# A block-sparse attention with a routed mixture of experts on one core: the third chunk's products one step later, PSUM halves alternating by pair, another opening

## The chip, the cores and the metric

One core of a Trainium2 chip (trn2) runs the whole program. The metric is the device time of one execution in microseconds (us); lower is better. Engines are named as the profile names them: PE is TensorE's matmul, PEld its weight load, DVE is VectorE, ACT is ScalarE, POOL is GpSimd, SP is SyncE, whose queue issues most DMAs.

## The reference: what is computed

Attention over 4 batches, 8 heads, 768 positions of 64 values, all float32. A block of 32 queries sees its own block of 32 keys and the two neighbours, the first and the last block, and 3 sampled blocks; the first and the last query block see everything. Then each of the 3072 rows (8 heads side by side, 512 values) is routed to one of 8 experts with a two-layer network.

```python
mask = np.abs(blk_i - blk_j) <= window
mask = mask | (blk_i == 0) | (blk_j == 0) | (blk_i == n_blocks - 1) | (blk_j == n_blocks - 1)
for qb in range(n_blocks):
    for kb in sampled_blocks[qb]:
        mask[qb * block:(qb + 1) * block, kb * block:(kb + 1) * block] = True
...
attn = np.exp(scores)
attn = attn / (np.sum(attn, axis=-1, keepdims=True) + 1e-09)
...
h = np.maximum(x_sorted[lo:hi] @ w1[e], 0.0)
y_sorted[lo:hi] = h @ w2[e]
return (gate_w[:, None] * y).astype(np.float32)
```

## The kernel before, in words

The program is one stream written out by hand for PE, DVE, POOL, ACT and SP. It opens with the loads and transposes of batch 0, then runs 48 attention steps, then the experts' tiles of 128 rows.

**Groups and steps.** A batch has six groups. Five (numbers 0 to 4) hold 128 query rows, which are two tiles of 64 (`ti` 0 and 1). The sixth, `GL`, comes first in each batch and has one tile of 64 rows, and beside it the 64 rows of the first and the last query block, which see all 768 keys. A group takes two steps, one for each half of the heads; a half is two pairs `pr` of heads, and `hh` is the head in a pair. So there are 4 x 6 x 2 = 48 steps, and the list `steps` gives their order.

**What a step does.** Step i makes the scores of its two pairs (`scores`, L357; for the rows that see everything L349) into a PSUM tile, ACT takes the exponential into a buffer `ea` (L362), DVE multiplies with the mask (L368, for `GL` L372). PE then transposes keys or queries of the next batch (`turn`, L178) and, in every second step, finished rows for the routing (`turn_out`, L469). Then come the products with V of the step before: `attend` (L388 on) for an ordinary group, `attend_last` for `GL`; both go through `product` (L383 to L390, the matmul is L386). After them come the routing logits (`logits`, L492) of a finished group, and `divide` on DVE (L445, L447, L451), which frees the PSUM bank.

**Chunks.** The keys of a tile lie in three chunks of 128: chunk 0 is the end blocks and the middle, chunks 1 and 2 are gathered. Their values of V come into the tile `around` (two sets, used in turn by `parity`), by POOL's indirect DMA from the copy `v_rows` in DRAM (`fetch_values(b, g, ti, ch)`, L525: `ch` 0 fills chunk 1, `ch` 1 fills chunk 2). Before most of them POOL copies one element of another tile (`not_before`, L539), so that the fetch is not issued too early. The rows of the two end blocks come by SP's DMA (`fetch_ends`, L535), rows of V of the own tile by copies on ACT and DVE (`place_values`, L544 and L545), keys by copies into `kr` and `xk` (`place_keys`, L567 and L570; `place_middle`, L551 and L552).

**PSUM halves.** A product has 64 output partitions: tile 0 writes partitions 0 to 63 of its bank, tile 1 partitions 64 to 127. In `attend` the two tiles alternate from one matmul to the next. In `GL` the 64 ordinary rows (three chunks) are half 0 and the rows that see everything (six chunks) half 1; `attend_last` alternates for three chunks and then runs the other three on half 1 alone. In batch 0 the rows that see everything are done in the opening, all on half 1 (`attend_all`, called four times), and the ordinary rows of `GL` later, all on half 0. There are two such banks (`ps_o`, 2 buffers); three score tiles (`ps_s`); seven buffers `ea`.

A float32 matmul of the program is two MATMUL records in the trace.

Of the kernel before, what the change touches and what calls it, by code (L numbers as in the profile page):

```python
# [17 lines left out]
def kernel(  # L18
# [11 lines left out]
    nc = tc.nc  # L30
# [351 lines left out]

    def product(b, g, pr, ti, hh, e, values, last):  # L383
        bank, begun = bank_of(b, g, pr)
        op = bank[:, : 4 * (D + 4)].rearrange("p (r h w) -> p r h w", r=2, h=2)
        nc.tensor.matmul(  # L386
            op[ti * D : (ti + 1) * D, pr % 2, hh, : D + 1], lhsT=e, rhs=values[:, (2 * pr + hh) * VW : (2 * pr + hh + 1) * VW],
            start=ti not in begun, stop=last, skip_group_check=True,  # L388
        )
        begun.add(ti)  # L390

    def attend(units_):

        for ch in range(3):
# [6 lines left out]
    def attend_all(b, pr, e, chunks):  # L401
        for c in chunks:
            for hh in range(2):
                product(b, GL, pr, 1, hh, e[:, hh, c * D : (c + 1) * D], sets[b][2][:, c, :], c == NCH - 1)

    def attend_last(b, pr, e_all, e_two):
        for ch in range(3):
            for hh in range(2):
                x = 3 * (pr % 2) + ch
                product(b, GL, pr, 0, hh, e_two[:, hh, x * D : (x + 1) * D], values_of(b, GL, 0, ch), ch == 2)  # L410
                if e_all is not None:
                    product(b, GL, pr, 1, hh, e_all[:, hh, ch * D : (ch + 1) * D], sets[b][2][:, ch, :], False)
        if e_all is not None:
            attend_all(b, pr, e_all, range(3, NCH))
# [19 lines left out]
    for pr in range(NPR):  # L434
        attend_all(0, pr, es[("all", pr)], range(NCH))
# [5 lines left out]
    def divide(b, g, half):  # L441
# [13 lines left out]
        if half == 1:  # L455
            for p, n, row in pieces(g):
                nc.sync.dma_start(x_d[b * S + row : b * S + row + n, :DM], xb[p : p + n, :])
# [26 lines left out]
    def logits(b, g, beside=None):  # L484
        xo = xos.pop((b, g))
        if beside is not None:
            lg = banks_of[beside][0][:, 4 * (D + 4) : 4 * (D + 4) + E]
        else:
            lg = ps_o.tile([P, E], F32, name="lgl", tag="op")[:]
        for c in range(DB):  # L490
            for j in range(2):
                nc.tensor.matmul(  # L492
                    lg[j * D : (j + 1) * D, :], lhsT=xo[:, c * P + j * D : c * P + (j + 1) * D], rhs=wg[:, c, :],
                    start=(c == 0), stop=(c == DB - 1), skip_group_check=True,
                )
# [812 lines left out]
    fetch_ends(0, GL)  # L1308
# [5 lines left out]
    fetch_ends(0, 0)  # L1314
# [6 lines left out]
    steps = [(b, g, half) for b in range(B) for g in order for half in range(2)]  # L1321
    for i, (b, g, half) in enumerate(steps):
# [15 lines left out]
        if two:  # L1338
# [17 lines left out]
        if half == 1 and i + 1 < len(steps):  # L1356
            not_before(mine[1][4][0:1, 0, 0:1])
            fetch_values(*steps[i + 1][:2], 0, 1)

        copy_turned = None  # L1360
        if b + 1 < B:
# [3 lines left out]
            if 2 <= here < 10:  # L1365
                copy_turned = turn(b + 1, (here - 2) // 2, here % 2, None, (here - 2) // 2 % 2)
                if 4 <= here < 8:
                    fill_next(b + 1, here)
# [3 lines left out]
        out_of = steps[i - 3][:2] if i >= 3 and half == 1 else None  # L1372
# [4 lines left out]
        if i > 0 and before[0][1] != GL:  # L1377
            attend(before)
        elif i > 0:
            for b_, g_, pr, e_all, e in before:  # L1380
                attend_last(b_, pr, e_all, e)
        if "gates" in rt:
            gate_weights()
        if out_of:
            logits(*out_of, beside=steps[i - 1])
            if out_of[1] == order[-1]:
                gate(out_of[0])
        if i > 0:
            divide(*steps[i - 1])
        early(late)  # L1390
        if half == 0 and nxt is not None:
# [195 lines left out]
```

## Time and profile before

| what | value |
|---|---|
| median of 3 runs | 640.93 us (637.01 to 645.84) |
| the profiled execution's own time | 638.06 us |
| its span | 636.3 us |
| granted TensorE clock over the span | 0.995 of full speed |
| PE busy / PEld busy | 608.2 us / 516.0 us |
| DVE / ACT / POOL busy | 315.6 / 231.9 / 193.8 us |

The span is cut in the prediction into the opening up to the first product (0 to 20.44 us), the attention steps (20.44 to 278.50 us) and the experts (278.50 to 629.3 us). A row of the timeline gives a start, a length, the engine, the line and the tiles, the count, and in brackets the idle time of the engine just before with what ended it. The starts of two neighbouring rows are the safe measure of how long PE takes for something, since the ends of matmuls are modelled.

### The profile page before, as it was taken

How to read it: one execution, taken by the hardware profiler on the slowest of the kernel's cores; microseconds unless marked ns; L12 is line 12 of the kernel's file. 1: busy time of each engine (PE TensorE's matmuls, PEld its weight loads, DVE VectorE, ACT ScalarE, POOL GpSimd, SP SyncE). 2: the span in 40 equal slices, each digit the busy share in tenths (PEclk: the TensorE clock that was granted, in tenths of full speed). 3: DMA queues.
4: the chain of work that ended last, by engine and by line, in shares of the span. 5: the costliest groups of instructions: out<-in, count | busy, mean ns of one | idle time of the engine just before them, and what ended most of it. 6: DMA issues, size and time to landing. Idle time of an engine off the chain costs nothing. (4 is left out here: it accounts for less than half of the span.)

```text
span 636.3 us, 20201 instructions
## 1 busy us (share of the span) xinstructions
PE 608.2 (96%) x8326; PEld 516.0 (81%) x8326; DVE 315.6 (50%) x1025; ACT 231.9 (36%) x456; POOL 193.8 (30%) x289
## 2 busy tenths in 40 slices
PE   6899999999999899999999999999999999999994
PEld 6888999998989899997777776877878787967862
DVE  7477767675778567635852485303190118203300
ACT  5376766665667577721111011111112111111110
POOL 2157745643456445720111221011401130020110
PEclk9899999999999999999999999999999999999999
DMA  8899966995696657899999999869998999769710
GB/s 264 207 193 246 288 162 153 255 261 154 136 247 206 184 147 250 261 322 369 338 305 313 344 388 336 303 229 379 396 399 281 365 399 399 291 205 407 299 40 20
DMA packets 125061, 170.86 MB, mean 269 GB/s; under 512 B 71236, under 2 KB 71237, under 8 KB 124934
## 3 DMA queue, kind: packets, MB, share of 16 engines
q1 hardware_dynamic: 114896, 137.61, 66.3%
q0 software_dynamic: 10000, 31.59, 16.0%
q8 instruction: 75, 1.23, 0.8%
q14 instruction: 52, 0.43, 0.2%
q10 hardware_dynamic: 38, 0.00, 0.0%
HBM read 150.11 MB, written 19.33 MB: 266 GB/s over the span
## 5 line engine op out<-in xcount | busy, mean ns | idle before, releaser
L525 POOL DMA_INDIRECT around<-v_rows,rows_of x88 | 100.0, 1136 | 55.3 <-DMA around<-v_rows 21.2
L362 ACT ACTIVATE ea<-s 128x768 f32<-128x768 f32 x104 | 83.6, 811 | 83.2 <-PE s L357 56.1
L1119 DVE STREAM_TRANSPOSE around<-xg 32x128 f32<-32x128 f32 x192 | 58.1, 303 | 86.9 <-DMA xg<-x_rows,gB 81.9
L1138 PEld LDWEIGHTS hp<-around,room 128*128 128x128 f32 x832 | 94.7, 192 | 3.9 <-issue 3.2
L1138 PE MATMUL hp<-around,room 128*128 128x128 f32 x832 | 96.8, 276 | 0.6 <-issue 0.3
L386 PE MATMUL op<-around,ea 128*64 128x65 f32 x2112 | 85.5, 224 | 8.8 <-DMA around<-v_rows,rows_of 5.1
L386 PEld LDWEIGHTS op<-around,ea 128*64 128x64 f32 x2112 | 75.4, 137 | 15.5 <-DMA around<-v_rows,rows_of 6.1
L368 DVE TENSOR_TENSOR ea<-ea,mask 128x768 f32<-128x768 f32 x80 | 74.6, 955 | 14.7 <-ACT ea L362 10.1
L1152 PE MATMUL zp<-room,kr 128*128 128x512 f32 x176 | 77.6, 594 | 0.0
L1145 ACT ACTIVATE kr<-hp 128x512 f32<-128x512 f32 x36 | 21.4, 597 | 116.0 <-PE hp L1138 98.3
L1172 POOL DMA_INDIRECT out_dram<-kr,sB x14 | 14.1, 1008 | 160.2 <-ACT kr L1162 97.9
L1152 PEld LDWEIGHTS zp<-room,kr 128*128 128x128 f32 x176 | 32.6, 190 | 37.2 <-issue 37.2
L357 PE MATMUL s<-other,kr 64*128 64x128 f32 x704 | 48.1, 272 | 0.3 <-issue 0.3
L357 PE MATMUL s<-room,kr 64*128 64x128 f32 x704 | 47.9, 272 | 0.2 <-issue 0.2
L1138 PEld LDWEIGHTS hp<-around,other 128*128 128x128 f32 x384 | 43.8, 192 | 2.3 <-issue 2.3
L1138 PE MATMUL hp<-around,other 128*128 128x128 f32 x384 | 44.3, 275 | 0.0
L357 PEld LDWEIGHTS s<-other,kr 64*128 64x128 f32 x704 | 43.7, 188 | 0.6 <-issue 0.6
L357 PEld LDWEIGHTS s<-room,kr 64*128 64x128 f32 x704 | 43.7, 188 | 0.0
L1250 DVE STREAM_TRANSPOSE ea<-ea 32x128 f32<-32x128 f32 x84 | 21.7, 285 | 30.9 <-DMA ea<-x_rows,gB 30.2
L1162 ACT ACTIVATE kr<-zp,xg 128x512 f32<-128x512 f32 x12 | 8.2, 687 | 74.9 <-PE zp L1152 74.9
L1152 PE MATMUL zp<-other,kr 128*128 128x512 f32 x80 | 35.3, 593 | 0.0
L1119 DVE STREAM_TRANSPOSE around<-kr 32x128 f32<-32x128 f32 x48 | 14.5, 302 | 36.3 <-PE hp L1138 34.9
(369 smaller groups left out, 831.2 us busy)
## 6 DMA issues: line engine op xcount, KB each, us to landing
room<-in_moe_w_dram SPq DMA_DIRECT2D x30, 2048.0 KB
other<-in_moe_w_dram SPq DMA_DIRECT2D x16, 2048.0 KB
room<-in_moe_w_dram SPq DMA_DIRECT2D x16, 512.0 KB
x_rows<-xb SPq DMA_DIRECT2D x20, 256.0 KB
room<-in_k_dram SPq DMA_DIRECT2D x24, 192.0 KB
room<-in_q_dram SPq DMA_DIRECT2D x24, 192.0 KB
v_rows<-room SPq DMA_DIRECT2D x12, 260.0 KB
v_rows<-other SPq DMA_DIRECT2D x12, 260.0 KB
```

The costliest lines, as they stand in the source:

```text
L357: nc.tensor.matmul(s[:, hh, a : a + P], lhsT=keys(r), rhs=moving, start=True, stop=True)
L362: nc.scalar.activation(e, s[:, :, : 6 * D], AF.Exp, scale=scale)
L368: nc.vector.tensor_tensor(e, e, m[:, None, :].to_broadcast([P, 2, 6 * D]), op=ALU.mult)
L386: nc.tensor.matmul(op[ti * D : (ti + 1) * D, pr % 2, hh, : D + 1], lhsT=e, rhs=values[:, (2 * pr + hh) * VW : (2 * pr + hh + 1) * VW], sta ...
L525: nc.gpsimd.indirect_dma_start(out=around[p0:, par, 1 + ti + 2 * ch, :], out_offset=None, in_=v_d[b][:, :], in_offset=bass.IndirectOffsetO ...
L1119: nc.vector.transpose(xT[d, :, t], xg[t, :DM].rearrange("p (c q) -> p c q", c=DB)[:, :, d])
L1138: nc.tensor.matmul(hp[:, m, :], lhsT=st[i]["w1"][:, c, fb * P : (fb + 1) * P], rhs=st[i]["xT"][:, c, :], start=(c == 0), stop=(c == DB - 1),)
L1145: nc.scalar.activation(hT[:, g * (FB // 2) : (g + 1) * (FB // 2), :], hp[:], AF.Relu)
L1152: nc.tensor.matmul(zp[:], lhsT=st[i]["hT"][:, fb, :], rhs=st[i]["w2"][:, fb, :], start=(fb == 0), stop=(fb == FB - 1),)
L1162: nc.scalar.activation(zo, zp[:], AF.Copy, scale=of_i)
L1172: ins = nc.gpsimd.indirect_dma_start(out=to[:, :], out_offset=bass.IndirectOffsetOnAxis(ap=at, axis=0), in_=rows, in_offset=None, bounds_c ...
L1250: nc.vector.transpose(xT_u[d, :, j * P + tq * 32 : j * P + (tq + 1) * 32], xg_u[t, j, :DM].rearrange("p (c q) -> p c q", c=DB)[:, :, d],)
```

## The change

Four things are changed.

- **The third chunk a step later.** For the steps where `in_two` holds (ordinary groups, but for the last step of each batch and the last four of all) `attend` is called twice: chunks 0 and 1 of step i-1 and then, one step later, chunk 2. In a step chunk 2 of step i-2 comes first, then chunks 0 and 1 of step i-1. A half is divided after its third chunk, so one step later; the finished rows are transposed at three steps behind the group's last (`out_at`), in even steps where it was odd ones. The fetch of chunk 2 of tile 0 is issued behind the products of step i-2, since it overwrites what they read.
- **Halves by pair.** In `GL` the ordinary rows of an odd pair now use half 1 and the rows that see everything half 0 (`side_of`), so that `in_turns` can alternate the halves to the end: 18 products on each side of a step for batches 1 to 3, 6 on each for batch 0, 12 on each for two pairs of the opening. The rows are written out to DRAM in two pieces of 256-byte runs each, and `logits` reads the swapped side.
- **The opening.** The scores of steps 0 to 3 come ahead of the products of steps 0 and 1, which both run in step 3. The transposes for batch 1 begin a step later.
- **End rows on chip.** For the first two groups the end blocks' values are copied by POOL from the loaded V, in place of four SP DMAs that read `v_rows` again.

```diff
+    def side_of(g, pr, ti):
+        return (ti + pr) % 2 if g == GL else ti
     def product(b, g, pr, ti, hh, e, values, last):
...
-            op[ti * D : (ti + 1) * D, pr % 2, hh, : D + 1], lhsT=e, ...
+            op[side * D : (side + 1) * D, pr % 2, hh, : D + 1], lhsT=e, ...
...
+    def in_turns(*sides):
+        for two in zip(*sides, strict=True):
+            for one in two:
+                product(*one)
+    def attend_last(units_):
+        sides = [[], []]
+        for b, _, pr, _, e_two in units_:
+            sides[pr % 2] += of_last(b, pr, e_two)
+        for b, _, pr, e_all, _ in units_:
+            if e_all is not None:
+                sides[1 - pr % 2] += of_all(b, pr, e_all)
+        in_turns(*sides)
...
-    for pr in range(NPR):
-        attend_all(0, pr, es[("all", pr)], range(NCH))
+    for half in range(2):
+        attend_first((2 * half, 2 * half + 1))
...
-    fetch_ends(0, GL)
+    for g in order[:2]:
+        for j in range(2):
+            nc.gpsimd.tensor_copy(
+                around[j * BLK : (j + 1) * BLK, parity(0, g), 0, :],
+                sets[0][2][j * (P - BLK) : j * (P - BLK) + BLK, j * (NCH - 1), :],
+            )
...
+    def in_two(n):
+        return steps[n][1] != GL and n % (2 * NG) != 2 * NG - 1 and n < len(steps) - 4
+    out_at = {}
+    for n in range(1, len(steps) - 2, 2):
+        out_at[n + (3 if n < len(steps) - 4 else 2)] = steps[n][:2]
...
-            if 2 <= here < 10:
+            turned_ = here - (2 if b else 3)
+            if 0 <= turned_ < 2 * NPR:
...
-        if i > 0 and before[0][1] != GL:
-            attend(before)
+        if i == 3:
+            for n in range(2):
+                attend_last(units_of[n])
+                divide(*steps[n])
...
+        if i > 1 and in_two(i - 2):
+            attend(units_of[i - 2], range(3) if i == 4 else (2,))
+            closed.append(i - 2)
+            spare = banks_of[steps[i - 2]][0]
+            if not out_of:
+                divide(*steps[i - 2])
+        if half == 1 and i + 1 < len(steps):
+            not_before(mine[1][4][0:1, 0, 0:1])
+            fetch_values(*steps[i + 1][:2], 0, 1)
+        if i > 3:
+            if steps[i - 1][1] == GL:
+                attend_last(units_of[i - 1])
+            else:
+                attend(units_of[i - 1], (0, 1) if in_two(i - 1) else (0, 1, 2))
```

How the instructions stand on PE at three places. A row is a line, the operation, the tiles, the output's size and the count; here one product counts once. First the opening, from the products of the rows that see everything (48) on; `s` are scores, `op` products, `tp` the transposes for batch 1. Minus is before, plus after.

```order
-L386 MATMUL op<-room,ea 64x65 x48
+L390 MATMUL op<-room,ea 64x65 x48
 L357 MATMUL s<-room,xk 128x128 x2
 L357 MATMUL s<-room,kr 128x128 x4
...
-L386 MATMUL op<-around,ea 64x65 x12
+L357 MATMUL s<-room,xk 128x128 x2
+L357 MATMUL s<-room,kr 128x128 x8
+L357 MATMUL s<-room,xk 128x128 x2
+L357 MATMUL s<-room,kr 128x128 x8
```

The 48 products keep their place and count (only which half comes after which is changed, which the rows don't show); behind the scores of steps 0 and 1 stood 12 products of step 0, and now the scores of step 2 stand there.

Second, the products of batch 0 at steps 4 to 6 with the semaphores that they wait for: DMASW are POOL's fetches, DVE the masks and divisions. Before, steps 5 and 6:

```order
L386 MATMUL op<-around,ea 64x65 x8
L386 MATMUL op<-around,ea 64x65 [waits DMASW6_49]
L386 MATMUL op<-around,ea 64x65 [waits DMASW7_49]
L386 MATMUL op<-around,ea 64x65 x6
L386 MATMUL op<-around,ea 64x65 [waits DMASW0_49]
L386 MATMUL op<-around,ea 64x65 [waits DMASW1_49]
L386 MATMUL op<-around,ea 64x65 x6
L492 MATMUL op<-wg,xo 64x8 [waits Activation_49]
```

Now, steps 5 and 6:

```order
L390 MATMUL op<-around,ea 64x65 x8
L390 MATMUL op<-around,ea 64x65 [waits DVE_49,PE_49]
L390 MATMUL op<-around,ea 64x65 x7
L390 MATMUL op<-around,ea 64x65 [waits DMASW6_49]
L390 MATMUL op<-around,ea 64x65 [waits DMASW7_49]
L390 MATMUL op<-around,ea 64x65 x6
...
L390 MATMUL op<-around,ea 64x65 [waits DMASW0_49]
L390 MATMUL op<-around,ea 64x65 [waits DMASW1_49]
L390 MATMUL op<-around,ea 64x65 x22
```

The two waits for the chunk 2 fetches (DMASW0 and DMASW1) stood 16 products behind the first of step 5; now they stand at the head of the products of step 6. In step 5 the ninth product, the first into the next bank, waits for DVE's division.

Third, the second `GL` step of batch 1; `other` is V of that batch for the rows that see everything, `around` the gathered V.

```order
-L386 MATMUL op<-around,ea 64x65
-L386 MATMUL op<-other,ea 64x65
-L386 MATMUL op<-around,ea 64x65
-L386 MATMUL op<-other,ea 64x65 x7
+L390 MATMUL op<-around,ea 64x65 x12
+L390 MATMUL op<-other,ea 64x65 x24
```

Before, each of the two pairs ended with six products in a row on one half (seven rows of `other`, the first of them still beside its partner); now all 36 alternate between the halves, the 12 of `around` first.

## Rows read from the trace of the kernel before

**Rows 1.** Stretches of the span: us, then busy us and count of PE, PEld, DVE, ACT, POOL, the granted PE clock, the DMA share and GB/s.

```profile
20.44:278.50 258.06, 244.60 (x5725) 233.34 (x5722) 173.32 (x522) 167.27 (x336) 136.90 (x210) 1.00 0.81 210
278.50:629.30 350.80, 348.46 (x2287) 268.93 (x2286) 127.27 (x461) 52.78 (x99) 51.34 (x54) 1.00 0.86 316
```

**Rows 2.** Who PE waited for over the whole span: us in total, times, longest us.

```profile
PE op L386 <- DMA around<-v_rows,rows_of: 5.1, 7, 1.0
PE op L386 <- issue: 3.5, 7, 1.2
```

**Rows 3.** Timeline of PE, two products of ordinary steps with what follows them (start, length).

```profile
110.56 1.62 PE L386 MATMUL op<-around,ea 128*64 128x65 f32 x48
112.11 0.49 PE L357 MATMUL s<-other,xk 64*128 64x128 f32 x4
```

**Rows 4.** The page's groups of the products: busy us, mean ns of one, idle before.

```profile
L386 PE MATMUL op<-around,ea 128*64 128x65 f32 x2112 | 85.5, 224 | 8.8 <-DMA around<-v_rows,rows_of 5.1
L386 PEld LDWEIGHTS op<-around,ea 128*64 128x64 f32 x2112 | 75.4, 137 | 15.5 <-DMA around<-v_rows,rows_of 6.1
```

**Rows 5.** Timeline of PE in batch 1, the products of the second `GL` step: the first, the last run, and what follows.

```profile
99.78 0.27 PE L386 MATMUL op<-around,ea 128*64 128x65 f32 x1
...
101.77 1.04 PE L386 MATMUL op<-other,ea 128*64 128x65 f32 x15
102.74 0.49 PE L357 MATMUL s<-other,xk 64*128 64x128 f32 x4
```

**Rows 6.** Timeline of PE, the opening.

```profile
20.44 2.84 PE L386 MATMUL op<-room,ea 128*64 128x65 f32 x26
24.50 4.30 PE L386 MATMUL op<-room,ea 128*64 128x65 f32 x70 [1.22 <-issue]
28.73 0.49 PE L357 MATMUL s<-room,xk 64*128 64x128 f32 x4
30.17 0.39 PE L357 MATMUL s<-room,xk 64*128 64x128 f32 x4
33.30 0.45 PE L386 MATMUL op<-around,ea 128*64 128x65 f32 x4 [1.13 <-DVE ea L372]
34.14 1.38 PE L386 MATMUL op<-around,ea 128*64 128x65 f32 x20 [0.39 <-DMA around<-v_rows,rows_of]
35.45 0.49 PE L357 MATMUL s<-room,xk 64*128 64x128 f32 x4
38.26 1.61 PE L386 MATMUL op<-around,ea 128*64 128x65 f32 x24
39.80 0.49 PE L357 MATMUL s<-room,xk 64*128 64x128 f32 x4
```

**Rows 7.** Single us of the opening, columns as in rows 1.

```profile
21.00:22.00 1.00, 1.00 (x12) 1.00 (x11) 1.00 (x7) 0.36 (x1) 0.00 (x0) 0.50 1.19 329
26.00:27.00 1.00, 1.00 (x21) 1.00 (x19) 0.00 (x0) 0.00 (x0) 0.00 (x0) 1.00 0.07 15
```

**Rows 8.** Timelines of ACT, DVE and POOL in the opening: the exponential of step 0, the key copies that step 2's scores need, the first fetch.

```profile
31.39 0.81 ACT L362 ACTIVATE ea<-s 128x768 f32<-128x768 f32 x1 [7.02 <-PE s L357]
33.66 0.29 DVE L570 COPY kr<-room 128x256 f32<-128x256 f32 x1
27.01 1.17 POOL L525 DMA_INDIRECT around<-v_rows,rows_of  x1 [21.21 <-DMA around<-v_rows]
```

**Rows 9.** Timeline of PE, the products that waited for a chunk 2 fetch after the opening.

```profile
54.73 0.62 PE L386 MATMUL op<-around,ea 128*64 128x65 f32 x13 [1.04 <-DMA around<-v_rows,rows_of]
117.59 0.62 PE L386 MATMUL op<-around,ea 128*64 128x65 f32 x13 [0.97 <-DMA around<-v_rows,rows_of]
137.59 0.62 PE L386 MATMUL op<-around,ea 128*64 128x65 f32 x13 [0.41 <-DMA around<-v_rows,rows_of]
182.66 0.62 PE L386 MATMUL op<-around,ea 128*64 128x65 f32 x13 [0.90 <-DMA around<-v_rows,rows_of]
212.47 0.62 PE L386 MATMUL op<-around,ea 128*64 128x65 f32 x13 [0.73 <-DMA around<-v_rows,rows_of]
274.94 0.62 PE L386 MATMUL op<-around,ea 128*64 128x65 f32 x13 [0.67 <-DMA around<-v_rows,rows_of]
```

**Rows 10.** Timeline of POOL and of PE: the fetch of chunk 2 of tile 1 that the first row of rows 9 waited for, and the products' start.

```profile
47.61 1.59 POOL L525 DMA_INDIRECT around<-v_rows,rows_of  x1 [0.15 <-issue]
52.42 1.27 PE L386 MATMUL op<-around,ea 128*64 128x65 f32 x34
```

**Rows 11.** Timelines of DVE and PE around two divisions: the last operation of a division, and the products of the next step.

```profile
61.00 0.42 DVE L451 TENSOR_TENSOR xb<-op,r 128x256 f32<-128x256 f32 x1
63.16 1.26 PE L386 MATMUL op<-around,ea 128*64 128x65 f32 x34
66.40 0.42 DVE L451 TENSOR_TENSOR xb<-op,r 128x256 f32<-128x256 f32 x1
68.61 1.81 PE L386 MATMUL op<-around,ea 128*64 128x65 f32 x48
```

**Rows 12.** Who PE waited for in the experts' stretch (278.5 to 629.3 us), all rows.

```profile
PE lay L1002 <- DVE orB L973: 0.4, 1, 0.4
PE hp L1138 <- issue: 0.3, 1, 0.3
PE hp L1138 <- ACT kr L1145: 0.3, 1, 0.3
```

More of the change, by code (lines that the diff above doesn't have):

```diff
@@ L385, in product, with attend @@
         op = bank[:, : 4 * (D + 4)].rearrange("p (r h w) -> p r h w", r=2, h=2)
+        side = side_of(g, pr, ti)
         nc.tensor.matmul(
-            op[ti * D : (ti + 1) * D, pr % 2, hh, : D + 1], lhsT=e, rhs=values[:, (2 * pr + hh) * VW : (2 * pr + hh + 1) * VW],
-            start=ti not in begun, stop=last, skip_group_check=True,
-        )
-        begun.add(ti)
-    def attend(units_):
-        for ch in range(3):
+            op[side * D : (side + 1) * D, pr % 2, hh, : D + 1], lhsT=e, rhs=values[:, (2 * pr + hh) * VW : (2 * pr + hh + 1) * VW],
+            start=side not in begun, stop=last, skip_group_check=True,
+        )
+        begun.add(side)
+    def attend(units_, chunks):
+        for ch in chunks:
             for b, g, pr, _, e in units_:
@@ L486, in logits @@
         if beside is not None:
-            lg = banks_of[beside][0][:, 4 * (D + 4) : 4 * (D + 4) + E]
+            lg = beside[:, 4 * (D + 4) : 4 * (D + 4) + E]
         else:
@@ L1337 @@
         two = half == 1 and i + 1 < len(steps) and len(tiles_of(steps[i + 1][1])) > 1
-        if two:
+        if two and i != 3:
             b_, g_, _ = steps[i + 1]
@@ L1384 @@
         if out_of:
-            logits(*out_of, beside=steps[i - 1])
+            logits(*out_of, beside=spare)
             if out_of[1] == order[-1]:
                 gate(out_of[0])
-        if i > 0:
-            divide(*steps[i - 1])
+        for n in closed:
+            if steps[n] in banks_of:
+                divide(*steps[n])
         early(late)
-        if half == 0 and nxt is not None:
-            if i >= 2:
+        if half == 0 and nxt is not None and i != 2:
+            if i > 2:
                 fetch_ends(*nxt[:2])
-                b_, g_, half_ = steps[i - 1]
+                b_, g_, half_ = steps[closed[0]]
                 not_before(sums[0:1, b_ * NG + g_, 4 * half_ : 4 * half_ + 1])
@@ L1409 @@
             gather(i - len(steps) + 3)
-        before = mine
     turn_x(0)
-    attend(before)
+    attend(units_of[i], range(3))
     divide(*steps[-1])
```

65 lines of the change are left out of this document (38 added, 27 removed).

## The prediction

> **What bounds the kernel now.** I read the stretches of the span first, since a share over the whole span mixes two programs. In the attention steps PE is busy 244.6 of 258.06 us, at the full clock, and no other engine is busy more than 173.3; in the experts' stretch PE is busy 348.5 of 350.8 us [rows 1]. So PE sets the end in both, and what the change is worth is PE time: idle time that goes, and work that takes less time. The reader should see next that the experts' stretch gives nothing back: PE waits there 1.0 us in all, never for a weight transfer [rows 12], and its fetches are released by the buffers that PE has read. I therefore carry a gain of the attention steps to the end one to one.
>
> The list of PE's waits shows how little idle time is named: 5.1 us in seven waits for the gathered V, and 3.5 us of "issue" in front of products, where PE waits for nothing the profile shows [rows 2]. If idle time were all, the change could win 5 us. The larger part must be found inside PE's busy time, and for that I read the timeline by starts. An ordinary step's products are 48 records, and from their start to the next group's is 112.11 - 110.56 = 1.55 us, 32.3 ns a record [rows 3], although one matmul lasts 224 ns and one weight load 137 [rows 4]: matmuls on alternating halves run beside each other. Where a run stays on one half a record costs more: 15 records in the 0.97 us to 102.74 [rows 5], and 70 in 28.73 - 24.50 = 4.23 us [rows 6], 60 to 65 ns. That factor of nearly two is what the second edit goes for.
>
> **The GL steps of batches 1 to 3.** Six steps have 72 records of products each. Now such a step takes 102.74 - 99.78 = 2.96 us [rows 5]; all alternating it takes 72 x 32.3 ns = 2.33. Gain 0.63 x 6 = 3.8 us. Bounds: nothing, if these alternations don't overlap as those of rows 3 do, and 4.5 if they reach 30 ns.
>
> **Batch 0's ordinary GL rows.** 24 records a step on one half: 35.45 - 34.14 = 1.31 us behind the wait for 20 of them, 39.80 - 38.26 = 1.54 us for all 24 [rows 6]. Alternating, 24 x 32.3 ns = 0.78. With about 1.5 for each now, the gain is 0.7 x 2 = 1.4 us.
>
> **The opening's 48 products.** 96 records from 20.44 to 28.73, 8.29 us, made of 26 records up to 23.28, a gap of 1.22, and 70 records [rows 6]. The first 26 ran at half the clock (granted 0.50 at 21 us, 1.00 at 26 us [rows 7]). If all alternated at the full clock with no gap they would take 3.1 us, a gain of 5.2. [...] If PE reaches the gap earlier and it still ends at 24.50, what is left is 70 x 32.3 ns = 2.3 us, end 26.8, gain 2.0. If the clock stays at half over those 70 the gain is gone. I take 2.5, near the fixed gap, since the other two ends both need something to change.
>
> **The opening's waits.** Before, PE idled 1.13 us for step 0's mask and 0.39 for a fetch [rows 6], some 1.5 us; step 0's and 1's products now stand behind the scores of steps 2 and 3, where mask and fetch are long done. What is late next is step 2's scores: they need keys that DVE copies behind step 0's mask. Before, these were done at 33.66 + 0.29 = 33.95, which is 5.2 us behind the start of step 0's scores (28.73), and nobody waited. Steps 0 and 1 give PE only about 3 us of scores (1.44 for step 0 [rows 6]). So a new wait of about 2 us; its lower bound is 1.1, if the exponential of step 0 (31.39 [rows 8], 1.2 us behind the start of the next scores) is prompter. I take 1.7. Net -0.2, a loss.
>
> **The third chunk.** Five waits of rows 9 go, from 54.73 to 212.47: 1.04 + 0.97 + 0.41 + 0.90 + 0.73 = 4.05 us. The sixth (274.94) is of the last four steps, which keep the old order. The fetch of the first was issued at 47.61 and was missed at 52.42 + 1.27 = 53.69, 6.1 us later; it was there at 54.7, 7.1 us [rows 9, 10]. One step more gives some 10.5 us. The fetch of tile 0's chunk 2 must now wait for products of the same step, but is used a step later too, so nothing is lost there. POOL, which waits in its place, has only element copies and the next fetch queued behind, both paced by later events. Bounds: 0 (each wait returns elsewhere) to 4.7.
>
> **Edits at nothing.** The four POOL copies of end rows lie ahead of the first fetch (27.01 [rows 8]), which waited for `v_rows` and not for POOL. SP gets four DMAs less there and three more for each `GL` group; SP is not waited for. The transposes of finished rows keep their number. Small lags inside runs (rows 11 has 48 records drawn out to 1.81) may give 0.5 us.
>
> **The sum.** 3.8 + 1.4 + 2.5 - 0.2 + 4.05 + 0.5 = 12.05, say 12 us. From the profiled execution's 638.06 that is 626. The median of the runs shown is 640.93, 2.9 us above, so the prediction is 629. The lower bounds of the terms add up to nearly nothing, the upper ones to 18.
>
> [...]
>
> **Rivals.**
>
> 1. The gain is half used up by new waits. The opening's gap moves along (0 of 2.5 us) and the new wait in front of step 2 is longer, or PE's "issue" gaps grow because it passes its instructions faster: of the 12 us some 5 to 6 remain, 635. For it: 3.5 us of such gaps in front of products [rows 2], one of them in the opening. Against: the number of instructions does not change.
> 2. Alternating more does not overlap more. Then 3.8 + 1.4 + 2.5 go, the third chunk's 4 us stay, 637. Against it stands rows 3, the same form of matmul.
> 3. The gain is made in the attention steps and lost in the experts, because weights must come 12 us sooner: 640. For it: the DMA share there is 0.86 at 316 GB/s [rows 1]. Against: no wait for weights now [rows 12], and the fetches before move forward too.
> 4. The other side: the banks. Two banks are held, and a bank that was freed a whole step before its next use is now freed in the step just before. Where the division is done at 61.00 + 0.42 = 61.4, the products that now need its bank come about 0.5 us behind 63.16; where it is done at 66.8, about 0.5 behind 68.61 [rows 11]. So 2.2 us are to spare. If DVE (or ACT's exponentials ahead of it) runs 3 us later than in these rows, PE waits 0.8 us in some 36 steps, 29 us, less the 12 gained: 658. The point from which this decides is a DVE 2.5 us later than now (0.33 x 36 = 12). Against: DVE is busy two thirds of the attention stretch [rows 1] and gets no new work.
>
> **How the numbers follow.** The forecast 0.64, rival 1 0.24, rival 2 0.03, rival 3 0.05, rival 4 0.04. The range is the forecast's 629 with the upper terms' end on one side (about 18 us gained less what the gap keeps: 620) and rival 1 and 2 on the other (638); about two in ten lie outside it. Faster by over 2%, which is about what a measurement of this kernel can tell, means below 628.1: just past the forecast. A bit under half of the first two cases ends there: 0.43. Slower by over 2% is rival 4 alone, 0.03; within 2% is the rest, 0.54.
>
> **What would show it.** Right: the list of PE's waits has no more than one or two waits for gathered V, under 1.5 us in all; the products of a `GL` step of batches 1 to 3 take 2.3 us from start to start; the first score of step 0 starts at 26 to 27 us; the experts begin about 12 us sooner, at 266 to 267, and take 351 us again. A wait of PE of 1 to 2 us for DVE's key copies stands before step 2's scores. Wrong: PE waiting for DVE's `sums` or `xb` in front of products in every step (rival 4); waits for weights behind 270 us (rival 3); 60 ns a record in the `GL` steps (rival 2).

## The result and the profile after

| | before | after |
|---|---|---|
| median of 20 runs each, us | 640.35 (634.85 to 647.45) | 643.29 (639.16 to 648.69) |
| ratio, 95% interval | | 1.0064, 1.0040 to 1.0089 |
| the profiled execution, its span, us | 638.06, 636.3 | 648.69, 646.9 |

The forecast was 629.0, in a range of 620 to 638. The kernel became slightly slower. Timed twice more, beside the second and the fourth lot of experiments, it gave 1.0060 (1.0027 to 1.0093) and 1.0001 (0.9973 to 1.0030). So it lies between no change and 0.6 per cent slower, and the gain of 12 us is missing in all three timings. The profiled execution is the longest of its 20 runs, so what is read from it alone is on the high side; two more traces of the same kernel come with the second and the fourth lot.

The stretches of the span, as in [rows 1] (the ninth column is the granted clock):

```profile
20.30:288.99 268.69, 244.69 (x5726) 231.92 (x5722) 175.14 (x522) 167.02 (x336) 140.05 (x213) 0.97 0.79 204
288.99:640.00 351.01, 348.55 (x2287) 268.88 (x2286) 127.27 (x461) 52.81 (x99) 51.33 (x54) 1.00 0.86 313
```

The experts take what they took. All 10.6 us were lost in the attention steps (268.69 against 258.06), and there the clock is no longer 1.00: a mean of 0.97 over 268.69 us is some 8 us of full clock not granted. Who PE waited for in that stretch, the longest rows (total, times, longest), to be read beside [rows 2]:

```profile
PE op L390 <- issue: 8.5, 18, 1.9
PE xr L495 <- issue: 3.9, 7, 1.1
PE s L349 <- issue: 3.1, 5, 1.7
PE tp L178 <- DMA room<-in_k_dram: 2.4, 2, 1.4
PE s L357 <- DVE kr L597: 2.2, 2, 2.1
PE s L357 <- issue: 2.2, 2, 1.1
PE op L390 <- DMA around<-v_rows,rows_of: 0.7, 1, 0.7
```

The waits for gathered V went from 5.1 to 0.7 us, as forecast. But "issue", idle time in which the profile shows nothing that PE waited for, is now 8.5 + 3.9 + 3.1 + 2.2 = 17.7 us. In the same stretch before it was 3.5 us in front of products [rows 2] and 3.2 in front of others, 6.7 in all, mostly here:

```profile
PE s L349 <- issue: 2.6, 5, 0.9
PE s L357 <- issue: 0.4, 2, 0.3
```

There are also waits for key loads, which SP issues. PE in the opening and in the second `GL` step of batch 1, as in [rows 6] and [rows 5]:

```profile
20.30 1.56 PE L390 MATMUL op<-room,ea 128*64 128x65 f32 x26
23.74 2.31 PE L390 MATMUL op<-room,ea 128*64 128x65 f32 x70 [1.87 <-issue]
25.98 0.49 PE L357 MATMUL s<-room,xk 64*128 64x128 f32 x4
...
31.46 1.45 PE L357 MATMUL s<-room,kr 64*128 64x128 f32 x12 [2.08 <-DVE kr L597]
...
37.67 1.62 PE L390 MATMUL op<-around,ea 128*64 128x65 f32 x48
39.22 0.49 PE L357 MATMUL s<-room,xk 64*128 64x128 f32 x4
```

```profile
96.00 0.92 PE L390 MATMUL op<-around,ea 128*64 128x65 f32 x24
96.75 1.57 PE L390 MATMUL op<-other,ea 128*64 128x65 f32 x48
98.25 0.49 PE L357 MATMUL s<-other,xk 64*128 64x128 f32 x4
```

Read the starts: the 48 opening products take 25.98 - 20.30 = 5.68 us (8.29 before), both steps' products of batch 0's `GL` rows 1.55 (2.85 for 44 of the 48 records), a `GL` step 2.25 (2.96). With alternating halves a record of the `GL` step takes 31 ns (2.25 us for 72), about what the prediction said (32.3). Behind the 2.08 us wait PE went on at half the clock, as single us show (the ninth column again):

```profile
31.00:32.00 1.00, 0.54 (x6) 0.54 (x8) 0.29 (x2) 0.95 (x2) 0.79 (x2) 0.86 1.22 233
32.00:33.00 1.00, 1.00 (x14) 1.00 (x12) 0.97 (x2) 1.00 (x3) 0.34 (x2) 0.50 1.23 217
```

By the trace's clock records the level was 0.50 for 3.41 us there, again for 3.41 us from 45.38 and from 86.34, and for 6.83 us from 277.49, each time behind idle time of PE (2.08, 1.87, 1.52 and 1.84 us within the 4 us before). At that level 16 score records took 1.70 us from their start to the next group's (280.08 to 281.78), and 0.89 at 1.00 (265.82 to 266.71). Not every gap brought it: behind the 1.66 us before 225.52, shown below, the clock stayed at 1.00. What sets it is not shown. Apart from these, each kernel's trace has one such stretch at its start, from 18.07 after and from 19.18 before, and one at its end, from 642.71 and from 633.58.

**Where the key loads went.** SP's queue in batch 1 and the two transposes that waited:

```profile
105.67 4.20 SPq L480 DMA_DIRECT2D x_rows<-xb  x6
...
111.55 1.64 SPq L546 DMA_DIRECT2D x_rows<-gw  x3
...
114.36 2.57 SPq L140 DMA_DIRECT2D room<-in_k_dram  x2
```

```profile
121.69 0.59 PE L178 MATMUL tp<-ident,room 64*128 64x64 f32 x12 [0.96 <-DMA room<-in_k_dram]
187.35 0.59 PE L178 MATMUL tp<-ident,room 64*128 64x64 f32 x12 [1.41 <-DMA room<-in_k_dram]
```

The same writes and the same key load before, where no transpose waited:

```profile
105.27 2.73 SPq L457 DMA_DIRECT2D x_rows<-xb  x3
...
110.50 2.79 SPq L140 DMA_DIRECT2D room<-in_k_dram  x2
```

In both traces SP issued these in the order of the program. Six writes of `GL` rows instead of three, and the routing weights (`gw`) of a group that is finished a step later, stand ahead of the key load: it is issued at 114.36 where it was issued at 110.50, for a transpose that comes at about the same time (121.69, before 120.96). (The pieces of these rows are 512 bytes long in the trace, not 256 as the section on the change has it.)

**Where "issue" comes from.** The second `GL` step of batch 3, after and then before, and the DMA queues of the after window 222.0 to 225.4 us (the page has 75 such packets of 16 KB for the whole program):

```profile
222.66 1.20 PE L349 MATMUL s<-other 64*64 64x64 f32 x65
225.52 0.69 PE L349 MATMUL s<-other 64*64 64x64 f32 x31 [1.66 <-issue]
```

```profile
218.99 1.20 PE L349 MATMUL s<-other 64*64 64x64 f32 x65
220.65 0.57 PE L349 MATMUL s<-other 64*64 64x64 f32 x23 [0.46 <-issue]
```

```profile
q8 instruction: 1, 0.02, 1.8%
```

Both stop at the same place. If PE's instructions are counted through the trace, weight loads included, it is number 9665 = 193 + 37 x 256; such a place is called a block border from here on. After, the packet of instructions started at 223.22, when PE had 0.6 us of work left, and PE went on at 225.52, 2.3 us behind the packet's start. Before, PE had needed 3.74 us for the 256 instructions up to the border, with the packet starting 1.8 us into them, and went on 2.4 us behind its start; after, it needed 3.17 us, with the packet 2.5 us into them. The opening's gap, 1.87 us after and 1.22 before, stands at a border too (193 + 2 x 256, within one), and ended 2.65 and 2.81 us behind the start of a 16 KB packet of instructions. That such gaps go with the number in PE's count is borne out by the run with 128 more instructions, in the third lot; that PE has no instruction to run in them is the author's reading, and the traces show the places and the times alone.

### The profile page after: what moved, and what is told of

It is laid out like the page before. It is cut to its first block, busy times and chain, and to the rows that moved or that the text cites. A ratio compares the mean times of both kernels' runs of the same rounds, so it can differ in the third digit from the quotient of the medians.

```text
span 646.9 us, 20217 instructions
## 1 busy us (share of the span) xinstructions
PE 608.1 (94%) x8326; PEld 514.4 (80%) x8326; DVE 317.7 (49%) x1025; ACT 231.7 (36%) x456; POOL 197.4 (31%) x293
## 5 line engine op out<-in xcount | busy, mean ns | idle before, releaser
L552 POOL DMA_INDIRECT around<-v_rows,rows_of x88 | 97.3, 1105 | 35.8 <-issue 18.2
L390 PE MATMUL op<-around,ea 128*64 128x65 f32 x2112 | 79.4, 227 | 7.5 <-issue 6.6
L390 PEld LDWEIGHTS op<-around,ea 128*64 128x64 f32 x2112 | 70.8, 140 | 13.2 <-issue 8.1
L357 PE MATMUL s<-room,kr 64*128 64x128 f32 x704 | 49.5, 278 | 3.3 <-DVE kr L597 2.2
L357 PE MATMUL s<-other,kr 64*128 64x128 f32 x704 | 50.4, 282 | 0.0
L357 PEld LDWEIGHTS s<-other,kr 64*128 64x128 f32 x704 | 46.4, 197 | 0.0
```

The source lines that it names most:

```text
L357: nc.tensor.matmul(s[:, hh, a : a + P], lhsT=keys(r), rhs=moving, start=True, stop=True)
L390: nc.tensor.matmul(op[side * D : (side + 1) * D, pr % 2, hh, : D + 1], lhsT=e, rhs=values[:, (2 * pr + hh) * VW : (2 * pr + hh + 1) * VW], ...
L552: nc.gpsimd.indirect_dma_start(out=around[p0:, par, 1 + ti + 2 * ch, :], out_offset=None, in_=v_d[b][:, :], in_offset=bass.IndirectOffsetO ...
```

## The experiments

Each lot ran on a chip of its own, and ratios are against the kernel before on that chip. A comparison across lots is therefore weaker than one within a lot. The first lot takes the change apart; its expectations name the causes then in view: the clock, SP's queue, instructions that run out, the new opening, and variation between executions.

**The kernel before, again** (no edit).

> The kernel before once more, for a second trace and its granted clock. Theory CLOCK (the change lost its gain by stretches at half clock, 24 us of the span at a mean clock of 0.981): the clock of before is 0.993 or more in all runs and its trace has no half-clock stretch between 23 and 620 us. Rival NOISE (every execution of either kernel has such stretches, the first profile of before was a lucky one): clocks of 0.98 to 0.99 here too, and idle time of PE in the attention steps well above the 12.9 us of the first profile. Ratio 1.000 either way.

Measured 0.9986 (0.9958 to 1.0014). Its trace has two stretches of 3.41 us at half the clock (from 18.54 and 32.19) and 5.9 us of waits for V. Its granted clock over the span was 0.981 to 0.994 in the 12 executions. So such stretches come in the kernel before too, and no single trace may be taken for the kernel.

**Pairs alone**: the halves of `side_of` and `in_turns` put into the kernel before, with the row writes in two pieces that they need and nothing else.

```diff
+            op[side * D : (side + 1) * D, ...
+    def in_turns(*sides): ...
```

> Before with the halves alternating by pair alone (opening's 48 products, batch 0's GL rows, GL steps of batches 1 to 3). By the sum of work this saves 3.8 + 1.4 + 2.5 = 7.7 us: theory WORK (work saved is time saved) 0.988. Theory INSTRUCTIONS (faster products only make PE run out of instructions, and the idle time lowers its clock): the steps of GL take 2.3 us but issue gaps grow by as much, 0.997 to 1.003. Theory OPENING (what was lost comes from the new order of the opening): 0.988 too.

Measured 0.9993 (0.9957 to 1.0028). In its trace, which is the longest of its 12 runs, the 48 products end at 25.61, and then step 0's products wait for gathered V:

```profile
36.74 1.13 PE L390 MATMUL op<-around,ea 128*64 128x65 f32 x16 [7.12 <-DMA around<-v_rows,rows_of]
```

Before, that wait was 0.39 us [rows 6]; in the trace of pairs and delay with the same old opening, below, it is 2.09 us. So in the old order time won by the opening's products goes, at least in part, into a longer wait for V. Over all steps this trace has 14.9 us of waits for V (5.9 in the trace above); where the gain goes in an execution near the median is not shown.

**The third chunk's delay alone.**

```diff
+        if i > 1 and in_two(i - 2):
+            attend(units_of[i - 2], (2,))
```

> Before with the third chunk a step later alone (with its later divisions and transposes of finished rows, and the later fetch), old opening, old halves. Theory WORK: the five waits for gathered V go, 0.9935 to 0.995. Theory QUEUE (SP's queue, with the row writes a step later, issues the key and query loads for the next batch later, and PE waits for them): 0.5 to 2.4 us of waits of the transposes for loads appear, 0.996 to 1.001. Theory OPENING: 0.994.

Measured 1.0103 (1.0055 to 1.0151) in six runs: the part that was forecast at -4 us costs 6.6 (3.5 to 9.6). None of the theories had it so high. The waits of its trace, 27 to 286 us:

```profile
PE op L386 <- issue: 5.2, 14, 1.0
PE s L349 <- issue: 2.9, 4, 1.7
PE s L357 <- issue: 2.2, 3, 1.7
PE tp L178 <- DMA room<-in_k_dram: 1.7, 1, 1.7
...
PE op L386 <- DMA around<-v_rows,rows_of: 0.3, 1, 0.3
```

The waits for V are gone (0.3 us); issue gaps (11 us) and a wait for keys came, without any of the pairs. That wait, at 65.44, is for keys of batch 1.

**Pairs and delay, with the old opening.**

```diff
+    fetch_ends(0, GL)
...
-        if i == 3:
-            for n in range(2):
-                attend_last(units_of[n])
-                divide(*steps[n])
...
-        if i > 3:
+        if i > 0:
```

> The changed kernel with the order of the opening as before (the products of steps 0 and 1 in steps 1 and 2, transposes a step earlier, end rows by DMA), but pairs and third chunk as changed. Theory OPENING: all the loss against the sum is in the opening, so 0.982 here. Theory WORK with QUEUE: 0.986. Theory INSTRUCTIONS: 0.996 to 1.004.

Measured 1.0036 (1.0010 to 1.0062). Within this lot, adding the pairs to the delay brings 0.7 per cent. With the new opening too, the whole change gave 1.0064, 1.0060 and 1.0001 in other lots, so the new opening does not clearly bring its share.

The second lot starts from the whole change.

**The changed kernel again.**

> The changed kernel itself, for a second trace. Its first trace had 22.0 us of idle PE in the attention steps and five stretches at half the clock (about 8 us lost to it), and was 5 us above the median of its own runs. If the idle time is in the program (it follows the order of the instructions), the second trace shows it at the same instructions: issue gaps of 12 to 16 us, waits for key loads of 2 to 3 us, 2 us before step 2's scores. If it is chance, the gaps stand elsewhere and come to less than 14 us in all. Ratio against the kernel before 1.004 to 1.009 either way.

Measured 1.0060 (1.0027 to 1.0093). Of its issue gaps, 12.2 us in the attention steps, most stand where they stood, so they are in the program. The two waits for key loads, expected at 2 to 3 us, were absent.

**The change without the third chunk's delay** (only step 2 keeps its place in the new opening).

```diff
-        return steps[n][1] != GL and n % (2 * NG) != 2 * NG - 1 and n < len(steps) - 4
+        return n == 2
...
```

> The change without its first part: every group's three chunks in one step again, with the pairs and the new opening. If the third chunk's delay is what costs (it alone gave 1.010), this is 0.6 to 1.2 per cent faster than the whole change: ratio 0.993 to 1.000 against the kernel before, work at full clock some 8 us less than before, waits for gathered V of 4 us back. If the opening is what costs, the ratio stays at 1.004 or above, since the pairs alone gave 0.999.

Measured 1.0013 (0.9978 to 1.0047), just past the expected 1.000. No issue gap at a block border is left in its trace, and the waits for V are back:

```profile
PE op L390 <- DMA around<-v_rows,rows_of: 4.9, 7, 1.1
```

**Step 2's second keys copied in step 0.**

```diff
+        if i == 0:
+            place_keys(b_, g_, 1)
-        if nxt is not None and half_ < len(tiles_of(g_)):
+        if nxt is not None and i != 1 and half_ < len(tiles_of(g_)):
```

> The change with step 2's second set of keys copied one step earlier, in step 0. The wait of 2.1 us before step 2's scores should go to under 0.3 us, and with it the stretch at half clock behind it (1.7 us). If both are carried to the end: ratio 3 to 4 us below the whole change's, 0.999 to 1.002. If the opening is bound by something behind it (the first gathers, the divisions), the wait moves there and the ratio stays at 1.004 to 1.008.

Measured 1.0038 (1.0006 to 1.0069), not told apart from the change (the medians of the two, 642.60 and 642.56, are equal), so the 0.999 to 1.002 for a gain that is carried to the end was missed. The wait and the half clock behind it went; in that place PE has small idle pieces, such as:

```profile
30.26 0.35 PE L357 MATMUL s<-room,xk 64*128 64x128 f32 x1 [0.28 <-issue]
```

Step 5 begins 2 us sooner (47.33, and 49.30 in the trace of the change on this chip), but this trace then has a gap of 2.40 us at a block border (from 82.17) and half clock behind it.

**Key and query loads of batches 2 and 3 a step earlier in SP's queue.**

```diff
-            if 4 <= here < 8:
-                fill_next(b + 1, here)
+            ahead = 1 if b else 0
+            if 4 <= here + ahead < 8:
+                fill_next(b + 1, here + ahead)
```

> The change with the key and query loads of batches 2 and 3 put one step earlier into the queue of SP. If SP's queue is what makes the transposes late, their waits (2.4 us in two places) go, and the half clock that may follow: ratio 0.4 to 0.6 per cent below the whole change's, 1.000 to 1.003. If those waits only stand in for others, the ratio stays at 1.004 to 1.008 and other waits of PE grow by 2 us.

Measured 1.0003 (0.9972 to 1.0034), median 639.27 against the change's 642.56. The time is as expected if SP's queue was at fault, and no transpose waits for a load. But in the change's own trace on this chip none waited for one either, so the wait that should have gone is not seen here.

Third lot. **The experts' first gathers a step later.**

```diff
-        if i >= len(steps) - 3:
+        if i >= len(steps) - 2:
...
-            gather(i - len(steps) + 3)
+            gather(i - len(steps) + 2)
+    gather(2)
```

> The changed kernel with the gathers of the first experts' rows (x_rows, by POOL) issued one step later each, so that they don't stand between the last two fetches of V. If POOL's indirect DMAs close behind each other are what makes PE idle in small pieces, the pieces in the step before the last (2.0 us in four or five, in all four traces with the third chunk late) go, and with them the half clock behind them: 2 to 4 us, ratio 0.999 to 1.003. If the transfers of weights or PE's own instructions make them, the pieces stay, ratio 1.004 to 1.008, or more if the later gathers are waited for.

Measured 1.0024 (0.9986 to 1.0062). This chip is faster with every kernel (before: 628.90), and its traces have none of the small pieces in any kernel; so the run can't tell what it was for. It shows a price: the experts wait for the later gather.

```profile
PE tpg L1154 <- DMA xg<-x_rows,gA: 1.5, 1, 1.5
```

In the attention steps its trace has the waits that the other two mends aim at:

```profile
PE tp L178 <- DMA room<-in_k_dram: 3.0, 2, 1.6
PE s L357 <- DVE kr L597: 1.4, 1, 1.4
```

**All three mends.**

> The changed kernel with three mends together: step 2's second keys copied in step 0, key and query loads of batches 2 and 3 a step earlier in SP's queue, the experts' first gathers a step later. If each loss is its own: 0.2 + 0.6 + 0.4 per cent off the whole change, ratio 0.992 to 0.996. If PE's idle time comes back in front of other instructions (its instruction blocks, other fetches), 0.998 to 1.002.

Measured 0.9937 (0.9901 to 0.9973), median 624.48 against 628.90: faster than the kernel before, within the range for losses that are each their own. Beside the run above, from which it differs by the early keys and the earlier loads alone, it is 0.9 per cent faster, and in its trace the waits of 4.4 us went to 0.6:

```profile
PE s L357 <- DVE kr L597: 0.4, 2, 0.2
...
PE tp L178 <- DMA room<-in_k_dram: 0.2, 1, 0.2
```

The whole change without mends was not timed on this chip.

**No delay, early keys of step 2, later gathers.**

> Pairs and new opening without the delay of the third chunk, with the early keys of step 2 and the later gathers. Without the third chunk's delay the trace has no issue gaps at block borders and its tail has no small pieces, so only the early keys can help: 1.4 us, ratio 0.998 to 1.001. If this is faster than the kernel with three mends, the third chunk's delay doesn't pay even when mended.

Measured 1.0009 (0.9977 to 1.0041). As expected in time, but 2.3 us of issue stand at block borders where none was expected. Its waits for V are 11.4 us in eleven places, and a transpose waits 1.4 us for a key load: that wait can come without the delay too.

**128 more instructions on PE at the start.**

```diff
+        for _ in range(32):
+            nc.tensor.matmul(idle[:32, 1, :1], lhsT=ident[:, :32], rhs=ident[:, :1], start=True, stop=True)
```

> The changed kernel with 128 more instructions on PE ahead of the loads' transposes (32 small products into a tile that nobody reads). One look at where PE idles with cause issue. If the long issue gaps (0.5 to 2.4 us) stand where PE comes to a new block of 256 of its own instructions, they stand again at instruction 193 + 256 k of PE's count, which is 128 instructions earlier in the program than now, and those between 'all' scores of the GL steps move or go. If they belong to the work at that place, they stay with the same instructions of the program, which then have the number 65 + 256 k. The time itself is not to be read closely: the added products take 1 to 3 us at the start, part of it in idle time.

One execution, 627.70. PE in a `GL` step of batch 1:

```profile
86.94 1.40 PE L351 MATMUL s<-other 64*64 64x64 f32 x80
89.71 0.46 PE L351 MATMUL s<-other 64*64 64x64 f32 x16 [1.38 <-issue]
```

All eight issue gaps of the attention steps stand at 193 + 256 k of PE's own count (this one is 3777), none at 65 + 256 k. They moved by 128 instructions through the program: in this trace these stops go with the number in PE's count, not with the work that stands there.

Fourth lot, one chip: **the change, the two mends (early keys of step 2, key loads earlier), and one execution of the kernel before.**

> The changed kernel a third time, beside the mended one on the same chip. If the small idle pieces behind POOL's indirect DMAs belong to the program, they are back (6 to 10 us in all); if they belong to the chip, they are here only if the kernel before shows them too. Ratio 1.002 to 1.008 against the kernel before; long issue gaps at instruction 193 + 256 k again, 3 to 7 us.

> The changed kernel with two mends: step 2's second keys copied in step 0, and the key and query loads of batches 2 and 3 one step earlier in SP's queue. If these two waits and the half clock behind them are what turned the gain round, ratio 0.992 to 0.998 and at least 0.5 per cent under the whole change on the same chip. If the later gathers were needed too, 0.998 to 1.004.

> The kernel before, for its trace on this chip. If the small issue pieces behind POOL's indirect DMAs are the chip's, they are here as often as in the change's trace from the same chip (per indirect DMA close behind another); issue gaps at block borders under 3 us.

Measured: the change 1.0001 (0.9973 to 1.0030), the two mends 0.9943 (0.9908 to 0.9977), the one execution 637.47. The first was expected at 1.002 to 1.008, a miss. The second is as expected, 0.6 per cent under the change on the same chip. The stretches from step 0's first scores to the experts, in this order before, after, mended:

```profile
27.86:278.47 250.61, 237.13 (x5628) 225.89 (x5626) 170.36 (x507) 163.99 (x328) 138.15 (x209) 1.00 0.81 211
```

```profile
25.44:277.79 252.35, 235.77 (x5628) 222.96 (x5626) 170.79 (x507) 163.37 (x328) 139.02 (x210) 0.99 0.81 210
```

```profile
26.28:274.25 247.97, 233.55 (x5628) 221.06 (x5626) 170.13 (x506) 163.38 (x328) 142.32 (x210) 1.00 0.81 213
```

Before and after, the longest rows of PE's waits in them:

```profile
PE op L386 <- DMA around<-v_rows,rows_of: 7.6, 9, 1.2
PE op L386 <- issue: 2.2, 6, 0.5
```

```profile
PE op L390 <- issue: 6.1, 15, 1.1
PE xr L495 <- issue: 2.2, 4, 1.1
PE s L349 <- issue: 1.9, 5, 0.6
PE op L390 <- DMA around<-v_rows,rows_of: 1.5, 1, 1.5
```

On one chip, 7.6 - 1.5 = 6.1 us of waits for V turned into 8.3 us more of issue (4.4 to 12.7 from 20 us on). The small pieces are there in both kernels of this chip, 3.7 us before and 8.5 after (the table below). The mended kernel has 11.1 us of issue, and in these steps no stretch at half clock and no wait for a load.

**The delay with the earlier loads.**

> The kernel before with the third chunk a step later and the key and query loads of batches 2 and 3 a step earlier. The delay alone gave 1.010. If SP's queue is how the delay loses, this is 0.998 to 1.003; if it loses through PE's instruction blocks and the tail, it stays at 1.005 to 1.010.

Measured 1.0008 (0.9983 to 1.0033), where the delay alone had 1.0103. The two ran on different chips, and the change itself gave 1.006 in two timings and 1.000 on this chip, so at most a part of the difference is the loads'. The one wait for a key load in the trace of the delay alone (1.73 us at 65.44) is for batch 1, whose loads this edit leaves where they were, and this trace has it still (1.45 us at 68.14). So the difference can't be that wait.

Fifth lot. **The two mends without the delay, and the earlier loads in the kernel before.**

> The two mends (keys of step 2 and key loads earlier) with pairs and new opening, but without the third chunk's delay. If the delay pays once mended, this stays at 0.998 to 1.002 against the kernel before, where the two mends with the delay gave 0.994, and waits for gathered V of 4 to 10 us stand in its trace. If pairs and opening alone make the gain, 0.993 to 0.996.

> The kernel before with the key and query loads of batches 2 and 3 one step earlier in SP's queue. Its transposes wait for no load in any trace, so 0.998 to 1.002 if the loads matter only because the third chunk's delay makes them late; 0.994 or less if they are worth something by themselves.

Measured 0.9996 (0.9963 to 1.0029) and 1.0066 (1.0037 to 1.0094). The first is as expected if the delay pays once mended; its waits for V are 11.6 us, above the 4 to 10 expected. The second was a miss: earlier loads cost the kernel before 4 us. Its trace has 10.3 us of waits for V; the longest:

```profile
182.23 1.02 PE L386 MATMUL op<-around,ea 128*64 128x65 f32 x13 [1.90 <-DMA around<-v_rows,rows_of]
```

Whether the loads make these waits isn't shown, as the kernel before has no trace on that chip. All three traces without the delay on the two faster chips have 10.3 to 11.6 us of them, one of these with the loads not moved.

**All traces together.** Issue gaps from the opening's first product to the experts, sorted by whether they stand at a block border (193 + 256 k of PE's count, within one):

| traces | at borders, us | elsewhere, us |
|---|---|---|
| before, three traces | 2.9, 0.3, 0.8 | 3.8, 3.7, 3.7 |
| pairs alone; earlier loads alone | 1.5; 2.1 | 4.9; 0 |
| change without the delay: as it is; with early keys and later gathers; with two mends | 0; 2.3; 1.8 | 7.9; 0; 0 |
| delay alone; with earlier loads | 5.6; 3.5 | 5.6; 5.3 |
| change, three traces | 8.5, 3.6, 4.2 | 9.2, 8.6, 8.5 |
| pairs and delay, old opening | 2.5 | 8.3 |
| change with early keys; earlier loads; both | 4.7; 3.8; 1.7 | 9.4; 10.3; 9.4 |
| change with later gathers; three mends; 128 instructions | 8.9; 6.9; 4.4 | 0; 0; 0 |

With the delay the borders cost 4.9 us in the mean of twelve traces, without it 1.5 in the mean of eight. Of the gaps elsewhere, 269 of 278 begin within 1.6 us behind the start of an indirect DMA of POOL, often where two follow each other closely; on the two chips of the third and fifth lot there are none. Stretches of 1.6 us behind such a start make up only some 55 per cent of these steps, so the two go together more often than by chance; what links them is not shown.

## Why the prediction was wrong

**What held.** The opening's products: 2.6 us (2.5 forecast), of which 0.76 are luck, since the gap in them ended at 23.74 and not at 24.50, where the forecast held it by estimate. Batch 0's `GL` rows: 1.3 (1.4). The `GL` steps: 6 x 0.71 = 4.3 (3.8). The waits for V: 5.1 - 0.7 = 4.4 (4.05, and 0.39 under the opening's waits). These four gains add up to 12.6 us, and they are in the trace. The new wait before step 2's scores: 2.08 us (about 2). The experts give nothing back and take 351 us again, so rival 3 is out; no wait for a division stands in the trace (rival 4), and alternation overlaps (rival 2). Of the signs that the prediction named, only one failed, the start of the experts: 288.99 in place of 266 to 267. None of them watched PE's "issue" or its clock.

**The step that failed** is that everything else stays: "Edits at nothing" and "The sum", which let no idle time of PE come in but the wait before step 2's scores, and let the clock stay. In the first pair of traces 258.06 became 268.69. So 10.6 + 12.6 = 23.2 us came in:

- issue, 6.7 to 17.7 us: 11.0, of which 0.65 is the opening's gap (1.22 to 1.87), already in its 2.6 us; 10.3 are left. The sum had "small lags" at -0.5. Rival 1 named this ("because it passes its instructions faster") but priced it, with a longer wait for keys, at about 6 us. The reason it gave against, that the number of instructions doesn't change, is true and doesn't help: in the pair of traces above what differs is the time that PE needed for the 256 instructions up to a border (3.74 and 3.17 us) and when in that time the packet started (1.8 and 2.5 us into it). That the delay shortens that time, since its waits go, fits the table but was not tried by itself.
- the clock: 0.97 in place of 1.00 over 268.69 us, 8. The prediction let it fall only in the opening. The granted clock fell to 0.50 behind some of the new idle time (for 3.41 us behind the 2.08 us before step 2's scores, which is 1.7 us of full clock), so that an idle us could cost more than itself.
- waits for key loads, 2.4. "SP is not waited for" was read from a trace in which its loads came in time; the delay of the divisions and the three more writes stand in the same queue.
- the waits for key copies, 2.2, nearly all of it before step 2's scores, less the 1.13 us for step 0's mask that went: 1.1. With the 0.39 us for a fetch, which is among the waits for V here, that is 0.7; the forecast was 0.2.

That is 21.8 of 23.2 us, with the clock's share only rough. This trace is the longest of 20 runs: on the chip of the fourth lot the same terms are 8.3 of issue, 1.7 of clock and 0.4 of key loads, and the change came out even.

**By parts**, in the first two lots: the delay costs 1.0 per cent by itself, the pairs bring 0 alone and 0.7 per cent beside the delay, the delay taken out of the whole change brings 0.5. So the term whose sign was wrong is "The third chunk": its 4 us of waits went and more came back, as issue, half clock and a wait for keys. Once the loads are moved (and step 2's keys), the whole change is 0.6 per cent faster than the kernel before (0.9943 and, with the gathers, 0.9937, on two chips). The same without the delay, on a third chip, gave 0.9996. That the delay pays once mended rests on this comparison across chips.

**Open.** Moving the loads, alone or with the early keys, brought 0.5 per cent in the second lot, 0.6 in the fourth and 0.9 in the third. In the third the traces show the waits that went (4.4 to 0.6 us). In the other two they don't: the waits for loads in the change's traces are 0 and 0.4 us, and only the fourth lot's pair shows fewer issue and half-clock us. By what way the loads act there (on the page the 75 packets of instructions take 0.8 per cent of the time of the same 16 DMA engines) was not tried. Nor was the reason why the pairs alone brought nothing, nor the link from POOL's indirect DMAs to the small pieces, which rests on their times alone.

## What to carry to other kernels

PE was busy 95 per cent of the attention steps before (244.6 of 258.06 us), and the 12.6 us won there were lost again, and more. So before a wait is taken away, look at the engine's idle time that has no releaser (issue was 6.7 us before and 17.7 after), where it stands, and what each queue will issue later. When work is finished a step later, follow every DMA queued behind it, also on queues that nobody waits for yet: here a key load that was issued 3.86 us later, at 114.36, was waited for by a transpose, 0.96 us. Try the parts of a change apart, and on more than one chip: here one part lost alone and another stood still, the whole won only once key loads and key copies had been put earlier, and one trace was 8 us from the next of the same kernel.

## What was not expected of the hardware

- PE idled up to 2.95 us (before 82.51, in the trace with the later gathers) at a border of 256 of its own instructions. About nine in ten of the some 90 such gaps in 20 traces, and 10 of 11 in the first pair, ended 2.2 to 3.0 us behind the start of a 16 KB packet of instructions; of all moments in these steps of the pair it is one in seven. The scores of the rows that see everything, 65 records in 1.20 us, pass 256 instructions sooner than the products, 48 in 1.55: with a weight load to each record that is some 2.4 us against 4.1, an estimate from these two figures.
- The chips of the five lots differ by up to 2 per cent with the kernel before (medians of 638.7 to 640.2 us on three, 627.9 to 628.9 on two), and only the three slower ones show the small issue pieces behind POOL's indirect DMAs.
